# A second copy of V in DRAM with a pair's heads side by side, and gathers of random blocks from it

## Chip, cores and metric

One core of a Trainium2 chip runs the whole kernel. The metric is the device time of one execution in microseconds, taken as the median of several runs. Lower is better.

## The reference

Block-sparse attention (4 sequences, 8 heads, 768 positions, 64 features, blocks of 32) is followed by a mixture of 8 experts with one expert per token. Cut to what matters here:

```python
# q, k, v: (4, 8, 768, 64); sampled_blocks: (24, 3)
scores = scale * q @ k.T
mask = (|blk_i - blk_j| <= 1) | first or last block as query or key
for qb in range(24):
    for kb in sampled_blocks[qb]:
        mask[qb's 32 rows, kb's 32 columns] = True
attn = softmax(where(mask, scores, -1e9))
x = (attn @ v) as (3072, 512)
expert = argmax(normalized(x) @ normalized(expert_emb).T / tau)
out[t] = gate[t] * relu(x[t] @ w1[expert]) @ w2[expert]
```

Each block of 32 queries so reads its neighbours, the first and last block, and three random blocks of keys and values that are known only when the kernel runs.

## The kernel before, in words

The attention runs first, over chunks of 128 queries. Two sequences form a pair of sequences (`a` is 0 or 1), and the two chunks at the same place of such a pair form a pair of chunks: 12 of them (`NS`), which the text calls pair 0 to pair 11. A step of the loop in `attention_fast` (from line 1382) handles one chunk, so a pair takes two steps, and there are steps 0 to 24. In step `s` TensorE makes the scores of chunk `s` (L580 and L583 for the near keys, L605 for the random ones) and weighs the values of the chunk of the step before: `weigh_far` (L660 with the tile `vg`) for the random blocks, `weigh_near` (L660 with `st`) for the near ones. `normalize` then divides on VectorE and writes the tile `x` (L725), of which there are three buffers; `route` writes `x` to `x_dram` (L881) some steps later.

The values stand in SBUF in six tiles `vt[0]` to `vt[5]`, each of 128 partitions, and each partition holds one position: 2 sequences by 8 heads by 65 numbers, the 65th a one that makes the row sum. The tiles are loaded for `a` = 0 at the start and overwritten for `a` = 1 during the loop (`load_v`, `values_at`).

The random blocks of values come by DMA. `gather_v` (L484) yields, for each pair of chunks, 12 gathers (6 for the pairs 0 and 11, whose chunk holds only two blocks of this kind): for each of the three random slots `r` and each of the four query blocks `g`, 32 positions of both sequences and all heads go into 32 partitions of `vg`. The input has the heads far apart, so each gather is 512 pieces of 256 bytes. The start of the block is a register that SP reads (`shifts`). `lanes_of` picks the partitions: for `r` = 0 and 1 every second one from 32 to 95, for `r` = 2 32 neighbours. `vg` has two buffers, so the gathers of pair p are issued in the steps 2p-2 and 2p-1, the first of them behind `weigh_far` of step 2p-2, and their first reader is `weigh_far` of step 2p+1.

All these DMAs are issued by SP, in the order of the program: `fetch_all` (L493) puts one load (queries L497, keys L497, values L497) before every second gather (L499) and the loads that are left behind them (L501). The writes of `x` to `x_dram` follow at the end of a step. A wait at the head of this queue holds all that is behind it.

After the attention the expert tiles follow (L1218 and L1231), whose weights SP loads (L1171). The SBUF that they go to becomes free when the attention has ended.

Of the kernel before, what the change touches and what calls it, by code (L numbers as in the profile page):

```python
# [12 lines left out]
F32 = mybir.dt.float32  # L13
# [8 lines left out]
B, H, S, D = 4, 8, 768, 64  # L22
BLK = 32
NB = S // BLK
NRAND = 3
NC = S // P
# [24 lines left out]
VW = H * (D + 1)  # L51
NI = NB - 2
NCH = B * NC
DUO = 2
NS = NCH // DUO
TURNS = [0, 2, 1, 3, *range(4, NCH)]
DEN_LOW, DEN_HIGH = 0.1, 1e10
NEG = -1.0e9
LGAT = 80
# [260 lines left out]
def pieces(c, shifted=True):  # L320

    if not shifted:
        return [(slice(0, P), c * P)]
    if c:
        return [(slice(0, P), c * P - BLK)]
    return [(slice(0, BLK), S - BLK), (slice(BLK, P), 0)]
# [56 lines left out]
def lanes_of(slot, g):  # L383

    if slot < 2:
        return slice(BLK + slot, NRAND * BLK, 2)
    return slice(0, BLK) if (slot + g) % 2 == 0 else slice(NRAND * BLK, P)
# [16 lines left out]
def pair_chunk(s):  # L404

    a, at = divmod(s, NC)
    return a, at if a == 0 else (at + 1) % NC


def place(n):  # L410

    a, c = pair_chunk(n // DUO)
    return DUO * a + n % DUO, c, n % DUO


def of_seq(src, a, i=None):

    if i is None:
        return src[DUO * a:DUO * (a + 1)].rearrange("i h s d -> s (i h) d")
    return src[DUO * a + i].rearrange("h s d -> s h d")  # L420


def in_pair(t, i=None):

    return t.rearrange("p i h e -> p (i h) e") if i is None else t[:, i]
# [46 lines left out]
def blocks_of(c):  # L472

    return range(2 if c == 0 else 0, NG)
# [9 lines left out]
def gather_v(k, s, i=None):  # L484

    a, c = pair_chunk(s)
    t, src = k.vg_ring[s % 2], of_seq(k.v, a, i)
    for r in range(NRAND):
        for g, shift in zip(blocks_of(c), shifts(k, mybir.EngineType.SP, r, c)):
            yield in_pair(t[lanes_of(r, g), g], i)[:, :, 0:D], src[bass.ds(shift, BLK)]  # L490


def fetch_all(k, gathers, loads):  # L493

    for i, (to, src) in enumerate(gathers):
        if i % 2 == 0 and loads:
            k.nc.sync.dma_start(out=loads[0][0], in_=loads[0][1])  # L497
            loads = loads[1:]
        k.nc.sync.dma_start(out=to, in_=src)  # L499
    for to, src in loads:  # L500
        k.nc.sync.dma_start(out=to, in_=src)  # L501
# [785 lines left out]
def after_step(n, b):  # L1287

    s = TURNS.index(DUO * b + 1) + 2
    steps = route(n, b)  # L1290
# [18 lines left out]
def attention_fast(n, ctx):  # L1309
# [66 lines left out]

    turning = {0: (4, 5), 1: (6, 7), 10: (8, 9), 11: (10, 11, 12), 12: (13, 14, 15)}
    keys_at = {2: (8, 9), 3: (10,), 4: (11,), 5: (12,), 6: (13,), 10: (14, 15)}
    values_at = {7: (0,), 8: (1,), 9: (2,), 11: (3,), 13: (4,), 15: (5,)}
    routed = {TURNS.index(DUO * b + 1) + 2: b for b in range(NS - 1)}  # L1380
    plan = []
    for s in range(NCH + 1):
        now, after, last, past = (TURNS[i] if 0 <= i < NCH else None for i in (s, s + 1, s - 1, s - 2))
        if s in routed:
            plan = after_step(n, routed[s]) + [p for p in plan if p[0] >= s]

        def planned(half):
            for when, part, what in plan:
                if (when, part) == (s, half):
                    what()  # L1390

        def keys_gathered():
            if after is not None:
                gather_k(n, after)

        ends = last is not None and place(last)[1] == 0
        late_keys = s in turning and s > 0
        if now is not None:
            score_near(n, now)
            score_far(n, now)  # L1400
        if not late_keys:
            keys_gathered()
        summed, n.parted = n.parted, None
        if summed is not None:
            sum_logits(n, last)
        if past is not None and past >= 2 * DUO:
            turn_x(n, past)
        elif past is not None and past % DUO:
            turn_x(n, past - 1)
            turn_x(n, past)  # L1410
        if ends:
            score_ends(n, last, 0)
            score_ends(n, last, 2)
        elif after is not None:
            turn_q(n, after)
        for g in turning.get(s, ()):
            turn_k(n, g)
        if late_keys:
            keys_gathered()
        planned(0)  # L1420
        if s == 0:
            stack_ends(n, 1, (0, 1), 0)
            stack(n, 1, 0)
            near_v(n, 1, range(NG), 0)
        elif s == 2:
            stack_ends(n, 0, (1,), 1)
            stack(n, 0, 1)
            near_v(n, 0, range(NG), 1)
        elif s == 3:
            stack_ends(n, 1, (0, 1), 1)  # L1430
            stack(n, 1, 1)
            near_v(n, 1, range(NG), 1)
        elif s == 4:
            stack_ends(n, 0, (0,))
            stack(n, 2)
        elif s % 2 and 5 <= s < NCH:
            if s // DUO + 1 in (NC, NC + 1):
                stack_ends(n, s // DUO + 1, (0, 1))
            stack(n, s // DUO + 1)
        if last is not None:  # L1440
            for part in range(2):
                weigh_far(n, last, part)
        if past is not None and past % DUO:
            n.parted = past // DUO
            part_logits(n, n.parted)
        if ends:
            weigh_ends(n, last, (0, 2))
            score_ends(n, last, 1)
            score_ends(n, last, 3)
            if after is not None:  # L1450
                turn_q(n, after)
        ahead, odd = s // DUO + 1, s % DUO
        loads, gathers = [], ()
        if s in (2, 3):
            loads += load_q(n, s)
        elif s >= 4 and odd and ahead + 1 < NS:
            loads += load_q(n, ahead + 1)
        if s == 3:
            gathers = gather_v(n, ahead)
        elif s >= 4 and ahead < NS:  # L1460
            if not odd:
                coming = gather_v(n, ahead)
            gathers = coming if odd else islice(coming, 6)
        if s == 3:
            near_v(n, 2, (0, 1))
        elif s == 4:
            near_v(n, 2, (2, 3))
            near_v(n, 3, (0, 1))
        elif s > 4 and ahead < NS:
            near_v(n, ahead, (2, 3) if odd else (0, 1))  # L1470
        for g in keys_at.get(s, ()):
            loads += load_k(n, g)
        for m in values_at.get(s, ()):
            loads += load_v(n, 1, m)
        fetch_all(n, gathers, loads)
        if ends:
            weigh_ends(n, last, (1, 3))
        if last is not None:
            weigh_near(n, last, 0)
            weigh_near(n, last, 1)  # L1480
            normalize(n, last, summed)
        if s == 0:
            build_consts(n)
            next(experts)
        if s == 1:
            next(experts)
            setup.close()
            n.dp = pool("dp_e", 1)
        if s == NC * (B - 1):
            right.close()  # L1490
            n.wp = n.wp_ctx.enter_context(n.tc.tile_pool(name="wp", bufs=1, side="right", reuse_waits="tile"))
        planned(1)
# [159 lines left out]
@with_exitstack  # L1652
def kernel(
    ctx: ExitStack,
    tc: tile.TileContext,
    q: bass.AP,
    k: bass.AP,
    v: bass.AP,
    sampled_blocks: bass.AP,
    moe_expert_emb: bass.AP,  # L1660
    moe_tau: bass.AP,
    moe_w1: bass.AP,
    moe_w2: bass.AP,
    out: bass.AP,
):
    assert tuple(q.shape) == (B, H, S, D) and tuple(out.shape) == (N, DM)
    assert tuple(moe_w1.shape) == (E, DM, F) and tuple(sampled_blocks.shape) == (NB, NRAND)
    n = Net()
    n.tc, n.nc = tc, tc.nc
    n.q, n.k, n.v, n.blocks, n.out = q, k, v, sampled_blocks, out  # L1670
    n.emb, n.tau, n.w1, n.w2 = moe_expert_emb, moe_tau, moe_w1, moe_w2
    n.loaded, n.vs, n.es, n.ets, n.sums, n.x, n.rows, n.weights = {}, {}, {}, {}, {}, {}, {}, {}

    n.raw, n.nsq, n.lg, n.turned_rows, n.relu = {}, {}, {}, {}, None
    n.kt, n.qt, n.kg, n.pac, n.pd, n.pb, n.av, n.xt = ({} for _ in range(8))
    n.exact = n.attending = False
    n.const = ctx.enter_context(tc.tile_pool(name="const", bufs=1))
    n.x_dram = tc.dram_tile([N + 1, XW], F32, name="x_dram")
    n.dens = n.const.tile([P, NCH, H], F32, name="dens")

    fast(n)
    todo = n.nc.values_load(n.todo[0:1, 0:1], min_val=0, max_val=2)
    with tc.If(todo > 0):
        more(n)
# [32 lines left out]
```

## Time and profile before

| what | value |
|---|---|
| median of 3 runs | 625.15 us (624.96 to 627.76) |
| the profiled execution's own time | 619.32 us |
| its span, from the first to the last instruction | 617.6 us |
| TensorE busy | 583.4 us, 94% of the span |
| VectorE, ScalarE, GpSimd busy | 244.6, 146.4, 244.6 us |
| granted TensorE clock | 0.992 of full speed |
| DMA packets | 177073, of which 135432 under 512 bytes |
| HBM read, written | 156.65 MB, 12.90 MB |

The span divides into the attention (to about 250 us) and the experts. "Busy" counts the time in which an engine has an instruction under way, and TensorE's matmuls overlap, so its share says little on small stalls; the waits and the rows in order of time say more. The DMA share is the mean over 16 DMA engines of the time that their packets take, and can pass 1 where packets overlap.

### The profile page before, as it was taken

What the parts mean: (1) busy time and instruction counts of PE and PEld (TensorE: products, weight loads), DVE (VectorE), ACT (ScalarE), POOL (GpSimd) and SP (SyncE); (2) the same over time, 40 slices, a digit from 0 to 9 for tenths busy, and PEclk for the clock granted to TensorE, in tenths of its full rate; (3) what the DMA queues carried; (4) which work ended last, traced back from release to release, by engine and by line L of the source; (5) the groups of instructions that cost most, each with busy time, mean ns of one, the idle gap of its engine ahead of it and who ended that gap; (6) DMA issues with size and microseconds to landing.
All of it is one profiled execution on the core that took longest, in us unless ns stands there. A gap on an engine that the chain in (4) does not pass through costs nothing.

```text
span 617.6 us, 18763 instructions
## 1 busy us (share of the span) xinstructions
PE 583.4 (94%) x7732; PEld 451.8 (73%) x7732; DVE 244.6 (40%) x743; ACT 146.4 (24%) x287; POOL 244.6 (40%) x474
## 2 busy tenths in 40 slices
PE   7699999998989988999999999999999999999995
PEld 5588888887888977777766777755777636777772
DVE  4424667577879962457211121112122121121110
ACT  2346555565645544100000000000000000000000
POOL 2728347446766330320333334443333333334432
PEclk9799999999999999999999999999999999999999
DMA  9998798999999851899999999998999998999611
GB/s 201 235 171 192 150 169 179 187 198 210 199 196 203 180 193 39 266 402 393 406 400 392 408 396 324 340 327 307 404 408 390 398 381 309 395 400 408 226 36 35
DMA packets 177073, 170.60 MB, mean 276 GB/s; under 512 B 135432, under 2 KB 137608, under 8 KB 174162
## 3 DMA queue, kind: packets, MB, share of 16 engines
q1 hardware_dynamic: 170706, 155.61, 81.2%
q0 software_dynamic: 5216, 13.43, 6.0%
q8 instruction: 63, 1.03, 0.7%
q10 hardware_dynamic: 1056, 0.26, 0.2%
q14 instruction: 32, 0.26, 0.1%
HBM read 156.65 MB, written 12.90 MB: 275 GB/s over the span
## 4 chain that ended last, share of the span: by engine, by line
PE 75%; DVE 9%; DMA 5%; SPq 4%; ACT 2%; issue 2%; POOL 1%; POOLq 0%; DVEq 0%; ACTq 0%
PE hp L1218 26%; PE yp L1231 25%; PE av L660 7%; PE dps L605 4%; SPq L499 3%; PE hp L1263 2%; PE yp L1283 2%; DVE qt L549 2%; PE ac L580 2%; DMA vg<-in_v_dram 2%; DMA w<-in_moe_w_dram 2%; PE ac L583 2%; PE kps L526 1%; PE xg_ps L740 1%; DVE xt L743 1%
## 5 line engine op out<-in xcount | busy, mean ns | idle before, releaser
L1218 PEld LDWEIGHTS hp<-xgt,w 128*128 128x128 f32 x1472 | 167.8, 192 | 10.9 <-issue 10.2
L1218 PE MATMUL hp<-xgt,w 128*128 128x128 f32 x1472 | 169.2, 275 | 0.3 <-DMA w<-in_moe_w_dram 0.3
L1231 PE MATMUL yp<-w,h 128*128 128x512 f32 x368 | 162.0, 592 | 0.0
L1231 PEld LDWEIGHTS yp<-w,h 128*128 128x128 f32 x368 | 68.1, 190 | 76.6 <-issue 76.3
L1142 POOL DMA_INDIRECT xg<-x_dram,quarter x88 | 89.2, 1014 | 32.3 <-issue 27.4
L1244 POOL DMA_INDIRECT out_dram<-y,slot_l x20 | 20.5, 1023 | 156.0 <-DVE y L1243 156.0
L1221 ACT ACTIVATE h<-hp 128x512 f32<-128x512 f32 x23 | 13.7, 597 | 283.1 <-PE hp L1218 280.2
L1225 DVE TENSOR_SCALAR h<-hp 128x512 f32<-128x512 f32 x23 | 15.9, 691 | 126.8 <-PE hp L1218 126.8
L562 POOL COPY kg<-kt 128x128 f32 x176 | 43.8, 299 | 33.5 <-ACT kt L528 23.1
L1243 DVE TENSOR_SCALAR y<-yp,gate 128x512 f32<-128x512 f32 x20 | 15.0, 751 | 102.2 <-PE yp L1231 90.1
L511 POOL COPY vg<-vt 32x1040 f32<-32x1040 f32 (+1 forms) x45 | 43.1, 958 | 21.4 <-PE av L660 14.5
L605 PEld LDWEIGHTS dps<-qt,kg 128*64 128x64 f32 x1408 | 46.7, 138 | 0.0
L605 PE MATMUL dps<-qt,kg 128*64 128x64 f32 x1408 | 45.8, 222 | 0.0
L583 PE MATMUL ac<-qt,kt 128*64 128x256 f32 (+1 forms) x192 | 42.4, 364 | 1.2 <-ACT kt L536 1.2
L580 PE MATMUL ac<-qt,kt 128*64 128x128 f32 x352 | 42.8, 273 | 0.3 <-DVE qt L549 0.3
L580 PEld LDWEIGHTS ac<-qt,kt 128*64 128x64 f32 x352 | 37.9, 137 | 0.6 <-issue 0.5
L549 DVE COPY qt<-yp 64x512 f32<-64x512 f32 x48 | 32.8, 683 | 12.1 <-PE yp L544 11.7
L610 ACT ACTIVATE pd<-dps,bias 128x256 f32<-128x256 f32 x88 | 34.7, 476 | 8.5 <-PE dps L605 8.3
L660 PE MATMUL av<-vg,pd 128*32 128x65 f32 x1408 | 27.5, 221 | 4.1 <-DMA vg<-in_v_dram 2.0
L660 PEld LDWEIGHTS av<-vg,pd 128*32 128x32 f32 x1408 | 22.3, 109 | 8.8 <-issue 4.4
L660 PEld LDWEIGHTS av<-st,pac 128*64 128x64 f32 x704 | 22.8, 137 | 5.8 <-issue 4.8
L730 ACT ACTIVATE pac<-x 128x512 f32<-128x512 f32 x24 | 15.1, 631 | 49.5 <-DVE x L725 49.5
(244 smaller groups left out, 629.4 us busy)
## 6 DMA issues: line engine op xcount, KB each, us to landing
w<-in_moe_w_dram SPq DMA_DIRECT2D x52, 2048.0 KB, 15.2
vg<-in_v_dram SPq DMA_DIRECT2D x132, 128.0 KB, 4.4
kraw<-in_k_dram SPq DMA_DIRECT2D x32, 192.0 KB, 4.6
x_dram<-x SPq DMA_DIRECT2D x10, 516.0 KB, 5.2
qraw<-in_q_dram SPq DMA_DIRECT2D x9, 512.0 KB, 6.2
w<-in_moe_w_dram SPq DMA_DIRECT2D x8, 512.0 KB, 5.1
vt<-in_v_dram SPq DMA_DIRECT2D x10, 256.0 KB, 5.7
vt<-in_v_dram SPq DMA_DIRECT2D x5, 512.0 KB, 6.6
```

The source lines that it names most:

```text
L511: k.nc.gpsimd.tensor_copy(out=k.vg_ring[s % 2][lanes_of(NRAND, g), g, which(i)], in_=k.vt[m][rows, which(i)])
L549: k.nc.vector.tensor_copy(out=t[rows, :, h], in_=ps[rows])
L562: copy(out=t[:, :, g, lanes_of(s, g)], in_=kt[:, :, bass.ds(shift, BLK)])
L580: nc.tensor.matmul(out[0:D, j, half], lhsT=kt[:, j, at:at + D], rhs=qt[:, j, :, D * half:D * (half + 1)], start=True, stop=True)
L583: nc.tensor.matmul(out[D:P, j, half:2].rearrange("p f h t -> p h f t"), lhsT=kt[:, j, S:S + D], rhs=qt[:, j, :, D * half:P].rearrange("p h ...
L605: nc.tensor.matmul(out[D * r:D * (r + 1), NG * j + g], lhsT=kg[:, j, g, D * r:D * (r + 1)], rhs=qt[:, j, :, cols], start=True, stop=True)
L610: nc.scalar.activation(e[:, :, g].rearrange("p j h t -> p j (h t)"), out.rearrange("p (j g) h t -> p j g (h t)", g=NG)[:, :, g], ACT.Exp, ...
L660: k.nc.tensor.matmul(av[lanes, h // NPAIR, h % NPAIR * P:h % NPAIR * P + D + 1], lhsT=lhsT, rhs=rhs, start=first[0], stop=last, skip_group ...
L1142: k.nc.gpsimd.indirect_dma_start(out=x[:, g], out_offset=None, in_=quarters, in_offset=bass.IndirectOffsetOnAxis(ap=k.quarter[:, g, t:t + ...
L1218: nc.tensor.matmul(hp[:, f, :], lhsT=w1[:, d, (f0 + f) * P:(f0 + f + 1) * P], rhs=xt[:, d, :], start=(d == 0), stop=(d == ND - 1))
L1231: nc.tensor.matmul(yp, lhsT=h[:, f, :], rhs=w2[:, f, :], start=(f == 0), stop=(f == NF - 1))
L1244: k.scattered = nc.gpsimd.indirect_dma_start(out=k.out[:, :], out_offset=bass.IndirectOffsetOnAxis(ap=slot, axis=0), in_=y[:, :], in_offse ...
```

## The change

A DRAM tile `joined[a]` is added for each pair of sequences: 768 rows of 2 x 8 x 65 numbers, 4160 bytes each. `join_v` writes it from the six tiles `vt`, whole rows with the ones in them: for `a` = 0 at the end of step 3's DMAs, for `a` = 1 in step 12 (tiles 0 to 2) and step 13 (tiles 3 to 5). Tile 0 takes two DMAs, each other tile one. For the pairs 3, 4, 5, 8, 9, 10 and 11 the gathers read 32 whole rows of `joined` in place of 512 pieces of the input; 6 x 12 + 6 = 78 of the 132 gathers are of these pairs. The pairs 0, 1, 2, 6 and 7 gather as before. The values of `a` = 1 are loaded earlier, tile 2 in step 8 (was 9), tile 3 in 9 (was 11), tile 4 in 10 (was 13), tile 5 in 11 (was 15).

```diff
+JOINED = (3, 4, 5, 8, 9, 10, 11)
@@ def gather_v
-            yield in_pair(t[lanes_of(r, g), g], i)[:, :, 0:D], src[bass.ds(shift, BLK)]
+            if s in JOINED:
+                yield t[lanes_of(r, g), g].rearrange("p i h e -> p (i h e)"), k.joined[a][bass.ds(shift, BLK)]
+            else:
+                yield in_pair(t[lanes_of(r, g), g], i)[:, :, 0:D], src[bass.ds(shift, BLK)]
+
+def join_v(k, a, m):
+    rows_of = k.vt[m].rearrange("p i h e -> p (i h e)")
+    return [(k.joined[a][lo:lo + rows.stop - rows.start], rows_of[rows]) for rows, lo in pieces(m)]
@@ def attention_fast
-    values_at = {7: (0,), 8: (1,), 9: (2,), 11: (3,), 13: (4,), 15: (5,)}
+    values_at = {7: (0,), 8: (1, 2), 9: (3,), 10: (4,), 11: (5,)}
+    joined_at = {3: (0, range(NC)), 12: (1, range(3)), 13: (1, range(3, NC))}
...
         fetch_all(n, gathers, loads)
+        if s in joined_at:
+            a, some = joined_at[s]
+            fetch_all(n, (), [piece for m in some for piece in join_v(n, a, m)])
...
+    n.joined = [tc.dram_tile([S, DUO * VW], F32, name=f"joined{a}") for a in range(B // DUO)]
```

## Rows read from the trace of the kernel before

**Rows 1.** Windows: busy us (instructions) of PE, PEld, DVE, ACT, POOL; PEclk, DMA share, GB/s.

```profile
94.00:231.00 137.00, 124.95 (x3279) 113.38 (x3281) 107.34 (x350) 76.20 (x160) 76.79 (x208) 1.00 0.91 195
270.00:617.00 347.00, 340.35 (x1930) 235.94 (x1928) 78.05 (x190) 15.52 (x26) 114.02 (x114) 1.00 0.90 342
```

**Rows 2.** Waits from 50 to 231 us: waiter, releaser, us in total, times, longest.

```profile
PEld av L660 <- DMA vg<-in_v_dram: 3.0, 5, 1.3
DVE x L725 <- DMA x_dram<-x: 2.7, 1, 2.7
PE av L660 <- DMA vg<-in_v_dram: 2.0, 3, 1.1
```

**Rows 3.** Timeline of PE: weigh_far of steps 7, 9, 13, 15 and 19 (start, us, ...).

```profile
94.40 1.11 PE L660 MATMUL av<-vg,pd 128*32 128x65 f32 x64
...
110.69 0.31 PE L660 MATMUL av<-vg,pd 128*32 128x65 f32 x4
112.11 1.21 PE L660 MATMUL av<-vg,pd 128*32 128x65 f32 x59 [1.10 <-DMA vg<-in_v_dram]
...
150.38 0.73 PE L660 MATMUL av<-vg,pd 128*32 128x65 f32 x4 [0.29 <-DMA vg<-in_v_dram]
...
167.29 1.20 PE L660 MATMUL av<-vg,pd 128*32 128x65 f32 x59 [0.57 <-DMA vg<-in_v_dram]
...
200.29 1.01 PE L660 MATMUL av<-vg,pd 128*32 128x65 f32 x57 [0.58 <-issue]
```

**Rows 4.** The page's DMA issues: KB of one, median us from issue to landing.

```profile
vg<-in_v_dram SPq DMA_DIRECT2D x132, 128.0 KB, 4.4
...
vt<-in_v_dram SPq DMA_DIRECT2D x5, 512.0 KB, 6.6
```

**Rows 5.** Timeline of SP's queue: six gathers of slots 0 and 1, three of slot 2.

```profile
149.19 4.74 SPq L499 DMA_DIRECT2D vg<-in_v_dram  x6
...
126.43 1.43 SPq L499 DMA_DIRECT2D vg<-in_v_dram  x3
```

**Rows 6.** Window of 1 us while SP issues only gathers (columns as Rows 1).

```profile
211.00:212.00 1.00, 1.00 (x17) 1.00 (x15) 0.93 (x4) 0.00 (x0) 0.00 (x0) 1.00 0.61 140
```

**Rows 7.** Timeline of SP's queue: the gather behind a load of queries, then of values.

```profile
155.25 1.48 SPq L499 DMA_DIRECT2D vg<-in_v_dram  x1
...
158.59 3.23 SPq L499 DMA_DIRECT2D vg<-in_v_dram  x1
```

**Rows 8.** Timeline of SP's queue from step 3's last gathers to step 6's end.

```profile
62.04 6.49 SPq L499 DMA_DIRECT2D vg<-in_v_dram  x8
68.92 0.40 SPq L497 DMA_DIRECT2D kraw<-in_k_dram  x1
72.00 1.46 SPq L499 DMA_DIRECT2D vg<-in_v_dram  x2
...
85.22 1.92 SPq L499 DMA_DIRECT2D vg<-in_v_dram  x2
...
95.72 2.03 SPq L881 DMA_DIRECT2D x_dram<-x  x2
```

**Rows 9.** DMA from 239 to 246 us, forty slices: one write to DRAM alone.

```profile
GB/s 0 0 0 0 0 0 0 0 0 0 12 389 366 366 377 389 377 366 319 47 24 24 12 94 0 0 0 0 0 0 0 0 0 0 0 0 0 0 0 0
...
x_dram<-x SPq DMA_DIRECT2D x1, 516.0 KB, 3.4
```

**Rows 10.** Timeline of DVE and SP: normalize in steps 7 and 15, a write.

```profile
101.30 0.69 DVE L725 TENSOR_TENSOR x<-av,inv 128x512 f32<-128x512 f32 x1 [2.73 <-DMA x_dram<-x]
...
163.71 1.56 SPq L881 DMA_DIRECT2D x_dram<-x  x1
...
170.55 0.69 DVE L725 TENSOR_TENSOR x<-av,inv 128x512 f32<-128x512 f32 x1
```

**Rows 11.** Waits of SP's queue over the whole span.

```profile
SPq L1171 <- PE av L660: 8.6, 1, 8.6
```

**Rows 12.** The page's line of DMA packets.

```profile
DMA packets 177073, 170.60 MB, mean 276 GB/s; under 512 B 135432, under 2 KB 137608, under 8 KB 174162
```

## The prediction, made before the changed kernel was built or run

> **What bounds the kernel now.** I read the windows by stage first. From 270 us on TensorE is busy for 340 of 347 us, at full granted clock, and the change touches nothing there. From 94 to 231 us it is busy for 125 of 137 us while the DMA engines are at 0.91 [rows 1], so the attention has two bounds that lie close together. Which one ends last is seen in the waits: in the attention TensorE waits on gathers of values for 3.0 us at the weight load and 2.0 us at the matmul (the same stalls, seen twice), and VectorE once for 2.7 us on a write of `x` [rows 2]. In order of time, `weigh_far` takes 1.11 us where nothing is late (step 7). In step 9 it begins at 110.69 us, stands still after four matmuls and ends 1.21 us after 112.11: 2.63 us, 1.5 too long. The steps 13, 15 and 19 show the same, with 1.4, 1.4 and 0.8 us lost from first matmul to last; one row of each stands there [rows 3]. These 5.1 us, and 0.8 us of TensorE in step 8 behind VectorE's wait, are all that a faster way to fetch V can give back. What is late there is not one transfer, since a gather lands 4.4 us after its issue [rows 4], but SP's queue: the gathers of pair 6, for step 13, go out until 147 us and are read from about 150 us on.
>
> **What a gather costs that queue.** Six gathers of slots 0 and 1, back to back, take 4.74 us, 0.79 each; three of slot 2, whose lanes are neighbours, 1.43 us, 0.54 each with the gap behind them [rows 5]. Both kinds move 512 pieces. So twelve that wait for nothing hold SP for 8 x 0.79 + 4 x 0.54 = 8.5 us. While SP does only this, the DMA engines are at 0.61 [rows 6]: there the issue sets the pace and not the bytes. Behind a load of queries the next gather holds SP for 1.48 us, behind one of values for 3.23 us [rows 7], for there the engines are full.
>
> **What a joined gather saves.** 32 rows instead of 512 pieces. Its lanes are those of before. Lower bound for its issue: 0.54 us, the price with neighbouring lanes; upper bound: 0.79, if every second lane is what costs. Eight a pair save 0 to 2.0 us; I take 1, between them. Further, the transfers of these gathers no longer stand in the engines ahead of the loads. A gather takes the engines about 0.61 x 0.79, 0.5 us; joined, 133 KB at the 400 GB/s or so of the largest slices of a write [rows 9] take 0.33 us. The wait behind a load of values should fall from 3.23 to about 2.1 us (two gathers stand between it and the queries), that of the write of `x` from 1.56 us [rows 10] to 0.5, that behind the queries by 0.3. Together S = 1 + 1.1 + 1.1 + 0.3 = 3.5 us of SP's time for each joined pair, with bounds of 1.4 (the last two alone) and 6 (an issue of 0.54, and no wait behind the values). A load that is not joined stays as it was, and the loads are the larger part of the packets.
>
> The Trainium skill (DMA: Bandwidth & Descriptors, section Specifications) gives 512 bytes as the least size for full rate. By it the gathers would be bound by their 256-byte pieces; the engines at 0.61 in [rows 6] speak against that for this queue, and what would follow from it is the first rival.
>
> **What the writes cost, and what stands behind them.** One write of 516 KB with nothing beside it moves at about 375 GB/s and lands 3.4 us after its issue, so 2.0 us are not bytes [rows 9]. The tile `joined[0]` is 768 x 4160 bytes = 3.19 MB: 8.5 us at that rate. Step 3's last gather leaves SP at 68.5 us [rows 8]. The seven writes follow, and the first joined gather, in step 4, reads what they write, so SP has to wait until they have landed: 68.5 + 2.0 + 8.5 + about 1 for what is still in the engines = 80 us, where before the first gather went at 72.0 us [rows 8]. Only one load of keys goes ahead of it. Everything else on SP, the gathers of the pairs 3 and 4, the queries, the keys, and the first two writes of `x`, stands behind this wait. So +8.0 us in the queue. For `joined[1]` it is 1.6 MB in each of the steps 12 and 13, 4.3 us each, and in step 14 a wait of some 6 us again, where by then no reader is near.
>
> **Moved loads.** Tiles 4 and 5 now come ahead of the last gathers of pair 6, before only behind them. At about 3.0 us each (3.23 less the next gather's own share, plus its own issue) that is +6.0 us for pair 6, and -3.0 us again by pair 7, from which tile 4 is gone. Tiles 2 and 3 change steps but not sides. The writes of `x` in steps 7, 9, 11 and 13 are moved by whatever stands ahead of them. The DMAs go by SP alone; TensorE, VectorE, ScalarE and GpSimd get no instruction more or less.
>
> **The sum, at each place where TensorE meets the queue.** How late SP is, against before:
> - Step 7: pair 3 has +8.0 - 3.5 = +4.5 us on its last gather. Before it was issued until 87.1 us [rows 8] and read at 94.40 [rows 3], so it lands near 95.5 us: +1 us.
> - Step 8: the write of `x` from step 6 has +8.0 - 1.5 x 3.5 = +2.8 us. VectorE already waited for it in step 7 until 101.30 us [rows 10], and TensorE was 0.8 us late behind that, so all of it is felt: +2.8 us, with the +1 inside it.
> - Step 9: pair 4 is +1 in the queue and TensorE +2.8, so the stall of 1.5 us is gone.
> - Step 13: +8.0 - 3 x 3.5 + 6.0 = +3.5 us; TensorE, now about 1.5 late by itself, waits to +3.5.
> - Step 15: +3.5 - 3.0 + 4.3 (tiles 0 to 2, which now stand ahead of pair 7's second half) = +4.8 us. The write of `x` behind it also has tiles 3 to 5 ahead of it; it had about 1.7 us to spare (issued from 163.71 us, needed at 170.55 [rows 10]), so some +5.
> - After that five pairs of joined gathers, without loads of values, leave SP time in hand: the stall of 0.8 us in step 19 goes.
>
> +5 - 0.8 = about +4 us at the end of the attention. The weights of the first experts wait for TensorE's last `weigh` there [rows 11], so the experts move by the same amount. In bounds: with S = 6 step 13 is at 8 - 18 + 6 = -4 and no step is late any more; with S = 1.4 step 15 is at 8 - 4.2 + 6 - 3 + 4.3 = +11.
>
> The profiled execution took 619.32 us (617.6 us of span and 1.7 around it): 623 us by this sum. The median of the runs is 625.15 us, 5.8 above it, and I move that by the same 4 us: 629 us.
>
> **Rivals.**
> 1. *Faster.* The queue is set by the 512 pieces after all, S is 5.5 or more, and the eight microseconds of step 3 are worked off before step 7. Then all stalls named above go: -5.1 - 0.8, about -6 and some of it given back, 620 us. It decides from S = 5.1, where 15.3 - 3S (step 15) turns negative. For it: the gathers behind values are held for 3.23 us, and after the change 39,936 of the 135,432 small packets [rows 12] are gone. Against it: [rows 5] and [rows 6], where the pace is the same with the engines 0.39 idle. This is also the time that the rule of the Trainium skill cited above would give, and the section Rules for kernel authors of the same page has a sentence for coalescing many small transfers.
> 2. *No change.* The wait for the writes and the moved loads cost what the gathers save, S between 4 and 5.1: 622 to 627 us. For it: SP was idle for 2.7 us ahead of 72.0 us anyhow [rows 8], and TensorE's lag hides what SP loses.
> 3. *Much slower.* The writes run at half of the rate of a single write, since keys and queries share the engines with them: +8.5 us at step 8 and +4 at step 15, of which most is felt, about +12, 637 us. For it: values landed after 6.6 us in the crowded queue [rows 4] against 3.4 for a larger write alone [rows 9].
> 4. *The change does not do what it says*: the rows of 4160 bytes are cut into pieces. Then the packet count would not fall by 36,000; the time would be that of rival 3. Little speaks for it.
>
> **Chances.** The forecast 0.42, rival 1 0.25, rival 2 0.20, rivals 3 and 4 0.13. A difference of under 0.5%, 3.1 us, is about what cannot be told from none in a measurement of this kernel. Part of the forecast's own range (626 to 634 us) lies within it, so: faster 0.25, same 0.27, slower 0.48. The range over the cases goes from 618 (all stalls gone, and a little more) to 638 us.
>
> **What would show it.** SP's queue should have no gather from about 72 to 80 us, and again some 6 us ahead of step 14's; if it has them at 72 us, the +8 is wrong. Joined gathers of slots 0 and 1 should follow each other at 0.55 to 0.8 us; at 0.54 and with the gather behind values under 1.5 us, S is near 6 and rival 1 wins. TensorE's waits on `vg` should move from step 9 to the steps 7 or 8, 13 and 15, and VectorE's on the write of `x` grow past 2.7 us. The packets under 512 bytes should be 95,496. The expert stage should keep its length; if it changes, I have missed something.

## The result, and the profile after

The changed kernel takes 632.12 us, median of 7 runs (630.33 to 635.83), against 625.15 us for the kernel before beside it (7 runs, 623.24 to 627.76). The ratio is 1.0138 with a 95% interval of 1.0109 to 1.0166, so about 8.6 us of 625 (6.8 to 10.4): slower, and about twice the 4 us that were forecast. The two medians alone lie 7.0 us apart, at the low end of that.

The two traces lie further apart than the medians. The profiled execution after took 635.5 us, at the slow end of its seven, and the one before 619.32, at the fast end. So 16 us lie between the traces, and a difference read from them is large by up to a factor of two, in its late part above all. 1.4 us are lost before step 4, where nothing of the change has run yet: `weigh_far` of step 4 begins at 72.31 us, before at 70.87. The granted clock of the first 60 us is 0.91, before 0.94. These rows of after and of before are windows (columns as in [rows 1]).

```profile
0.00:60.00 60.00, 47.52 (x978) 41.10 (x980) 25.52 (x94) 25.14 (x46) 28.45 (x99) 0.91 0.96 200
```

```profile
0.00:60.00 60.00, 50.14 (x1007) 43.28 (x1008) 25.52 (x94) 25.50 (x46) 30.15 (x100) 0.94 0.97 200
```

I take 1.4 us off the lateness of every later step, and call what is left "net". It compares with a kernel before that starts as late; SP itself is only 0.1 us late at the end of step 3 (68.65 us below, 68.53 before).

The change does what it says. The page of after (compare [rows 4, 12]) has 78 gathers of 130 KB and, of the writes, ten of a whole tile, and the small packets fell to 95,720; 95,496 were forecast.

```profile
DMA packets 141393, 177.15 MB, mean 280 GB/s; under 512 B 95720, under 2 KB 97896, under 8 KB 138482
...
vg<-joined SPq DMA_DIRECT2D x78, 130.0 KB
...
joined<-vt SPq DMA_DIRECT2D x10, 520.0 KB
```

SP's queue in order of time (compare [rows 8]; start, us held, what was issued). It is held by the seven writes for 7.3 us, issues one load of keys, and then stands until the first joined gather at 81.34 us, where before it went on at 72.00.

```profile
68.65 7.33 SPq L511 DMA_DIRECT2D joined<-vt  x7
76.79 0.40 SPq L507 DMA_DIRECT2D kraw<-in_k_dram  x1
81.34 1.19 SPq L509 DMA_DIRECT2D vg<-joined  x2
...
93.63 1.09 SPq L509 DMA_DIRECT2D vg<-joined  x2
...
101.17 1.01 SPq L891 DMA_DIRECT2D x_dram<-x  x2
...
160.77 3.29 SPq L511 DMA_DIRECT2D joined<-vt  x4
...
173.60 1.93 SPq L511 DMA_DIRECT2D joined<-vt  x3
175.64 1.13 SPq L891 DMA_DIRECT2D x_dram<-x  x1
180.53 1.83 SPq L509 DMA_DIRECT2D vg<-joined  x2
```

Who waits (60 to 250 us; us in total, times, longest; compare [rows 2]): TensorE for gathers, 6.2 us at the matmul where it was 2.0; VectorE for the write of `x`; and, new, SP for the landing of the copy.

```profile
PE av L670 <- DMA vg<-in_v_dram: 5.1, 7, 1.8
PE av L670 <- DMA vg<-joined: 1.1, 1, 1.1
...
PEld av L670 <- DMA vg<-joined: 1.9, 4, 1.2
...
DVE x L735 <- DMA x_dram<-x: 4.4, 2, 3.6
...
SPq L509 <- DMA joined<-vt: 7.2, 3, 3.5
```

In order of time, `weigh_far` of the steps 7, 13 and 15 (first and last rows of each; compare [rows 3]). Step 7 was on time before and now lasts from 96.45 to 100.45 us. Step 15 begins at 174.60 us and ends at 178.38, 7.2 and 8.4 us net later than before.

```profile
96.45 0.69 PE L670 MATMUL av<-vg,pd 128*32 128x65 f32 x4 [0.53 <-issue]
98.21 2.13 PE L670 MATMUL av<-vg,pd 128*32 128x65 f32 x59 [1.07 <-DMA vg<-joined]
...
156.37 0.69 PE L670 MATMUL av<-vg,pd 128*32 128x65 f32 x4 [1.55 <-DMA vg<-in_v_dram]
...
157.98 1.01 PE L670 MATMUL av<-vg,pd 128*32 128x65 f32 x57 [0.26 <-DMA vg<-in_v_dram]
...
174.60 0.27 PE L670 MATMUL av<-vg,pd 128*32 128x65 f32 x2 [1.83 <-DMA vg<-in_v_dram]
...
176.52 1.75 PE L670 MATMUL av<-vg,pd 128*32 128x65 f32 x57 [0.27 <-DMA vg<-in_v_dram]
```

The last row holds something that the forecast has no term for: 57 matmuls take 1.75 us where 57 take 1.01 in step 13. The windows of 5 us show why: in the third column from the end the granted clock is below 1 here. In four of the windows with a lower clock it comes behind a window in which TensorE was idle for 1.5 to 2 us; behind the one from 155 us, with 2.1 us idle, it does not.

```profile
95.00:100.00 5.00, 3.28 (x70) 2.64 (x73) 4.42 (x14) 3.61 (x7) 2.67 (x11) 0.81 0.95 219
100.00:105.00 5.00, 5.00 (x111) 4.19 (x102) 0.37 (x2) 0.37 (x1) 4.63 (x13) 0.85 0.71 177
...
155.00:160.00 5.00, 2.90 (x92) 2.06 (x94) 2.10 (x7) 2.87 (x6) 2.29 (x8) 1.00 0.86 225
160.00:165.00 5.00, 5.00 (x116) 4.93 (x113) 3.75 (x12) 2.53 (x6) 4.88 (x10) 1.00 0.89 237
...
170.00:175.00 5.00, 3.04 (x67) 2.59 (x63) 4.19 (x16) 4.23 (x8) 0.97 (x5) 1.00 0.74 154
175.00:180.00 5.00, 4.03 (x86) 2.98 (x88) 0.17 (x1) 0.82 (x2) 4.29 (x11) 0.66 1.06 379
...
235.00:240.00 5.00, 5.00 (x140) 4.79 (x140) 1.59 (x7) 0.18 (x2) 0.00 (x0) 0.70 0.45 178
...
255.00:260.00 5.00, 5.00 (x176) 4.64 (x172) 0.55 (x2) 1.62 (x2) 0.00 (x0) 0.66 0.13 48
```

In the trace of before no window of 5 us from 85 to 290 us has a clock below 1.00; it is the only one of the traces here without such a window. The last `weigh_far` begins at 256.66 us, before at 242.74: 12.5 us net. The experts add 1.3 us, one window of theirs being at 0.74.

### The profile page after: what moved, and what is told of

The parts are those of the page before. It is cut to its first block, busy times and chain, and to the rows that moved or that the text cites. A ratio compares the mean times of both kernels' runs of the same rounds, so it can differ in the third digit from the quotient of the medians.

```text
span 633.7 us, 18780 instructions
## 1 busy us (share of the span) xinstructions
PE 590.7 (93%) x7732; PEld 457.6 (72%) x7732; DVE 240.8 (38%) x743; ACT 146.0 (23%) x287; POOL 244.5 (39%) x474
## 2 busy tenths in 40 slices
DMA packets 141393, 177.15 MB, mean 280 GB/s; under 512 B 95720, under 2 KB 97896, under 8 KB 138482
## 4 chain that ended last, share of the span: by engine, by line
PE 77%; SPq 7%; DVE 4%; DMA 4%; issue 3%; ACT 2%; POOL 1%; another core or an unknown queue 1%; POOLq 0%; DVEq 0%; ACTq 0%
PE hp L1228 25%; PE yp L1241 24%; PE av L670 8%; SPq L509 5%; PE dps L615 4%; PE hp L1273 2%; PE yp L1293 2%; PE ac L590 2%; PE ac L593 2%; PE xg_ps L750 1%; DMA w<-in_moe_w_dram 1%; PE bps L646 1%; PE kps L536 1%; DVE qt L559 1%; ACT pb L648 1%
## 5 line engine op out<-in xcount | busy, mean ns | idle before, releaser
L1228 PEld LDWEIGHTS hp<-xgt,w 128*128 128x128 f32 x1472 | 169.4, 193 | 11.4 <-issue 10.2
L670 PE MATMUL av<-vg,pd 128*32 128x65 f32 x1408 | 31.2, 235 | 8.1 <-DMA vg<-in_v_dram 5.1
L559 DVE COPY qt<-yp 64x512 f32<-64x512 f32 x48 | 32.8, 684 | 11.8 <-PE yp L554 11.4
L620 ACT ACTIVATE pd<-dps,bias 128x256 f32<-128x256 f32 x88 | 34.6, 476 | 9.0 <-PE dps L615 9.0
L670 PEld LDWEIGHTS av<-vg,pd 128*32 128x32 f32 x1408 | 25.3, 118 | 13.5 <-issue 8.5
L670 PE MATMUL av<-st,pac 128*64 128x65 f32 x704 | 27.5, 230 | 0.8 <-issue 0.7
```

The lines of the kernel that those rows point to most:

```text
L559: k.nc.vector.tensor_copy(out=t[rows, :, h], in_=ps[rows])
L620: nc.scalar.activation(e[:, :, g].rearrange("p j h t -> p j (h t)"), out.rearrange("p (j g) h t -> p j g (h t)", g=NG)[:, :, g], ACT.Exp, ...
L670: k.nc.tensor.matmul(av[lanes, h // NPAIR, h % NPAIR * P:h % NPAIR * P + D + 1], lhsT=lhsT, rhs=rhs, start=first[0], stop=last, skip_group ...
L1228: nc.tensor.matmul(hp[:, f, :], lhsT=w1[:, d, (f0 + f) * P:(f0 + f + 1) * P], rhs=xt[:, d, :], start=(d == 0), stop=(d == ND - 1))
```

## Experiments

Each ran beside the kernel before; lateness in us is the ratio's excess times the median of before on that chip. The plain difference of the medians departs from it by up to 1.8 us. I began with a theory Q: SP's queue is a sum, TensorE waits for the queue's order, and the forecast missed only sizes in it. Its rivals are named in each expectation.

### The moved loads alone (e1_moved)

```diff
-    values_at = {7: (0,), 8: (1,), 9: (2,), 11: (3,), 13: (4,), 15: (5,)}
+    values_at = {7: (0,), 8: (1, 2), 9: (3,), 10: (4,), 11: (5,)}
```

> The kernel before with one part of the change alone: the values of a = 1 are loaded at the earlier steps; no writes to joined, no joined gathers. Theory Q (SP's queue in order: a load of 2048 pieces holds it for some 3 us, so tile 2 now stands ahead of pair 5's last gathers and the tiles 4 and 5 ahead of pair 6's): slower than before by 4 to 5 us, about 0.7%, with TensorE waiting on vg some 2 us in step 11 and until 4 us later than before in step 13. Rival B (what costs is the 6.4 MB that the writes put on the DMA engines): no byte more, so within 1 us of before.

Measured: 627.01 us against 623.10, ratio 1.0058 (1.0025 to 1.0091), 3.6 us slower. As Q has it. Step 9 lasts 2.81 us, much as before (2.68), but the steps 11 and 13 last 2.37 and 3.46 (before 1.11 and 2.58): there is a load more ahead of pair 5 too, which the forecast denied.

### The writes and the moved loads, no reader (e2_writes)

```diff
-JOINED = (3, 4, 5, 8, 9, 10, 11)
+JOINED = ()
```

> The changed kernel with JOINED empty: the writes to joined and the moved loads stand, all gathers read the input as before, so nobody waits for the writes. Theory Q: the writes hold SP for about 7 us in step 3 and 3 us each in the steps 12 and 13 by their issue alone, and the 1.5 to 2.5 us a pair that joined gathers gave are gone: 10 to 14 us slower than before, more than the changed kernel's 8.6. Rival W (the wait for the landing of the writes is what costs, 9 us at step 4): without it the time falls to that of the moved loads alone, 4 to 5 us over before.

Measured: 635.07 us, ratio 1.0197 (1.0163 to 1.0232), 12.3 us slower. As Q has it. So all that the 78 joined gathers give, with the waits that they bring, is 12.3 less 8.6, some 4 us, with about 2 us of uncertainty on either number.

### No one waits for the copy (e3_no_wait)

```diff
-JOINED = (3, 4, 5, 8, 9, 10, 11)
+JOINED = (4, 5, 9, 10, 11)
```

> The changed kernel with JOINED = (4, 5, 9, 10, 11): the pairs 3 and 8, whose gathers come right behind the writes, read the input, so SP has two steps for other work before it needs the written rows and the wait for their landing should be gone. Theory Q: the 4.2 and 3.8 us in which SP stood still go, and the 1.7 us that pair 3 saved go with them: 4 to 6 us over before instead of 8.6. Rival B (bytes on the engines): as the changed kernel, 8 to 9 us over before.

Measured: 631.93 us, ratio 1.0165 (1.0104 to 1.0225), 10.3 us slower. Q falls here. SP no longer waits for the landing and issues pair 3's first gather at 77.30 us in place of 81.34, but the first writes of `x` come at 100.20, only 1 us earlier than in the changed kernel, of which 0.7 is an earlier start (the seven writes at 67.91 against 68.65). Its SP queue:

```profile
67.91 7.25 SPq L511 DMA_DIRECT2D joined<-vt  x7
75.95 1.11 SPq L507 DMA_DIRECT2D kraw<-in_k_dram  x1
77.30 1.83 SPq L509 DMA_DIRECT2D vg<-in_v_dram  x2
...
100.20 1.00 SPq L891 DMA_DIRECT2D x_dram<-x  x2
```

The wait that the forecast priced at 8 us is not where the time goes: without it the queue is late anyway. Two things changed at once here, since the pairs 3 and 8 lost their savings with their wait, and 10.3 us (6.5 to 14.0) cannot be told from 8.6; the writes without any reader, further down, are the cleaner test.

### The first half alone (e4_first)

```diff
-JOINED = (3, 4, 5, 8, 9, 10, 11)
+JOINED = (3, 4, 5)
-    values_at = {7: (0,), 8: (1, 2), 9: (3,), 10: (4,), 11: (5,)}
-    joined_at = {3: (0, range(NC)), 12: (1, range(3)), 13: (1, range(3, NC))}
+    values_at = {7: (0,), 8: (1,), 9: (2,), 11: (3,), 13: (4,), 15: (5,)}
+    joined_at = {3: (0, range(NC))}
```

> Only the first half of the change: joined for a = 0, its writes in step 3, the pairs 3, 4 and 5 gathered from it; the loads of a = 1 where they were before, nothing joined for a = 1. Theory Q: TensorE is 3 to 4 us late at step 8 (SP waits until about 81 us and the first writes of x come behind that), but the pairs 5 to 7 are no later than before, so the stalls of the steps 9, 13 and 15 are covered by it: 1 to 3 us over before. Rival B: about half of the 8.6 us, 4 us, as half of the bytes are written.

Measured: 628.82 us, ratio 1.0083 (1.0046 to 1.0119), 5.2 us slower, more than either had it. The stalls of the steps 9 to 19 shrink (13 and 15 last 1.11 us each, before 2.58 and 2.53), as three joined pairs should make them, and yet the loss of the steps 7 and 8 is not won back.

### The second half alone (e5_second)

```diff
-JOINED = (3, 4, 5, 8, 9, 10, 11)
+JOINED = (8, 9, 10, 11)
-    joined_at = {3: (0, range(NC)), 12: (1, range(3)), 13: (1, range(3, NC))}
+    joined_at = {12: (1, range(3)), 13: (1, range(3, NC))}
```

> The moved loads and the second half of the change: joined for a = 1 alone, written in the steps 12 and 13, the pairs 8 to 11 gathered from it; pairs 3 to 5 read the input and nothing is written in step 3. Theory Q, mended by the first runs (what counts is how late SP is at the places where TensorE needs it; the writes hold SP by their bytes whether or not anyone waits for them): the moved loads alone gave 3.9 us; the writes of tiles 0 to 2 put pair 7 about 4 us later, those of 3 to 5 the write of x behind it, so TensorE is 3 to 5 us later in step 15 than with the moved loads alone: 6 to 9 us over before, granted clock about 0.981. Rival A (the parts add up: 8.6 for all, less 5.2 for the first half, less 3.9 for the moved loads): the second half costs nothing, 3 to 4.5 us over before.

Measured: 631.08 us against 623.92, ratio 1.0100 (1.0052 to 1.0148), 6.2 us slower. The halves give 5.2 + 6.2 = 11.4 us, the whole 8.6. That a step that is late already hides what comes late with it would explain the rest, but each of these numbers is uncertain by 2 to 3 us, so whether the halves add up is not shown.

### The copy written from another queue (e6_act_queue, e7_act_45)

Both issue the writes from ScalarE's queue; the second joins only the pairs 4 and 5, with the loads of before.

```diff
-            fetch_all(n, (), [piece for m in some for piece in join_v(n, a, m)])
+            for piece in [piece for m in some for piece in join_v(n, a, m)]:
+                nc.scalar.dma_start(out=piece[0], in_=piece[1])
```

> The changed kernel with the writes to joined issued from ScalarE's queue instead of SP's; everything else as changed, so the joined gathers of the pairs 3 and 8 still wait until the rows have landed. Theory Q (hold): SP is free of the 7 us of issue in step 3 but waits for the landing at step 4 as before, to about 80 us; in the steps 12 and 13 it is free and pair 7 and the writes of x come 3 to 5 us earlier than in the changed kernel: 4 to 7 us over before. Rival B (bytes): the engines carry the same 6.4 MB at the same places, 8 to 9 us over before.

Measured: 634.86 us, ratio 1.0173 (1.0124 to 1.0223), 10.8 us slower (7.7 to 13.9), no better than the change. The first writes of `x` go out at 102.29 us.

```profile
102.29 1.00 SPq L891 DMA_DIRECT2D x_dram<-x  x2
```

> First half without hold and without wait: joined for a = 0 is written from ScalarE's queue in step 3, only the pairs 4 and 5 are gathered from it, two steps later, and the loads of a = 1 stand where they were before. SP neither issues the writes nor waits for them; the engines still carry the 3.2 MB. Theory Q: the two pairs' savings (1.5 to 2.5 us each) come without their price, SP is earlier by 2 to 4 us in the steps 9 to 13, and the time is 0 to 4 us under before. Rival B (bytes): the 8.5 us of the write stand in the engines ahead of pair 3 and of the first writes of x, TensorE is 3 us or more late in step 8, and the time is 2 to 4 us over before.

Measured: 629.77 us, ratio 1.0090 (1.0059 to 1.0121), 5.6 us slower. The same as the first half from SP (5.2). But neither kernel frees SP. ScalarE issues the copy from 63.00 us on, ahead of step 3's gathers, and SP stands 8.6 us between a load of keys and its next gather, at 69.11 us. That gather reads the input, and yet it waits for the copy (SP's waits, 60 to 250 us, of the second kernel; 12.4 in the first):

```profile
SPq L509 <- DMA joined<-vt: 8.9, 2, 8.4
```

The cause lies in how these kernels count their DMAs. In the traces, in the semaphore numbers of the issuing instructions, the DMAs of SP and ScalarE tell their landing on the same eight semaphores (counters that an engine can wait for), and each is issued only when the last one on its semaphore has landed. The gather at 69.11 us takes the semaphore of the third write of the copy, which ScalarE issued at 63.87 us and which landed at 68.98. From SP alone the eight go round in order, and in the kernel before SP waits for no DMA between 60 and 250 us. So the theory's condition, an SP that neither issues nor waits, did not hold, and these two runs do not decide between Q and B.

### Another load from another queue (e9_q_act)

The kernel before, with the loads of queries from step 5 on issued by ScalarE.

```diff
-            loads += load_q(n, ahead + 1)
+            queries = load_q(n, ahead + 1)
+        for to, src in queries:
+            nc.scalar.dma_start(out=to, in_=src)
```

> The kernel before, nothing of the change; the loads of queries from step 5 on are issued from ScalarE's queue instead of SP's. If the place where the time is lost is SP's queue in order, so that a load of 2048 pieces holds the gathers behind it, SP gains 1.5 to 2.5 us per pair, TensorE's stalls of the steps 9, 13, 15 and 19 shrink, and the kernel is 2 to 6 us faster than before, with a higher granted clock (0.990). If the engines are the bound, the bytes are the same and the time stays within 1.5 us.

Measured: 632.15 us against 623.92, ratio 1.0103 (1.0052 to 1.0154), 6.4 us slower; neither had that. The chain of waits of that stretch (start, us, what) shows the queries' transfer and the write of `x` that comes in behind it; VectorE waits 8.5 us for that write, before 2.7.

```profile
96.69 6.56 DMA qraw<-in_q_dram
103.25 0.02 issue
103.27 3.50 DMA x_dram<-x
```

SP's waits (60 to 250 us) show that this is again the shared semaphore: SP holds back gathers and the write of `x`, which need nothing from the queries, until queries of ScalarE's queue have landed, nine times and for 34.6 us in all.

```profile
SPq L499 <- DMA qraw<-in_q_dram: 24.9, 7, 7.1
...
SPq L501 <- DMA qraw<-in_q_dram: 5.7, 1, 5.7
...
SPq L881 <- DMA qraw<-in_q_dram: 4.0, 1, 4.0
```

So a second queue didn't open a free path in these kernels, and the three runs don't tell what one would give whose DMAs SP need not wait for. The Trainium skill (DMA: Bandwidth & Descriptors, section "Issuing engines are not separate DMA queues") says that DMAs of all engines run on the same 16 DMA engines and interleave, and that issuing from several only saves issue time. No run here isolates that.

### The gathers without their price (e10_gain, e12_no_write)

Both read fixed rows of one tile that one DMA writes; the first has the loads of before, the second the moved loads of the change.

```diff
-                yield t[lanes_of(r, g), g].rearrange("p i h e -> p (i h e)"), k.joined[a][bass.ds(shift, BLK)]
+                yield t[lanes_of(r, g), g].rearrange("p i h e -> p (i h e)"), k.joined[0][g * BLK:(g + 1) * BLK]
-    joined_at = {3: (0, range(NC)), 12: (1, range(3)), 13: (1, range(3, NC))}
+    joined_at = {3: (0, (1,))}
```

> The joined gathers without their price: the loads are those of the kernel before, one DMA of one tile (128 rows, 0.53 MB) stands where seven stood, and the gathers of the pairs 3, 4, 5, 8, 9, 10 and 11 read 32 fixed rows of that tile. It leaves out the copying of V and the addresses of the blocks, so other numbers are weighed and other experts picked; the attention's steps are what to compare. Theory Q (a joined gather frees SP's queue by some 2.5 us a pair, as the gaps between the last gathers of each pair in the changed kernel say, and the queue's order is what TensorE waits for): the stalls of the steps 9, 13, 15 and 19 go, last weigh_far 4 to 6 us earlier than before, 4 to 6 us faster. Theory E (the other loads keep the engines as busy, so that the gathers' gain is not felt): within 1.5 us of before, the stalls of the steps 13 and 15 still over 2 us long from first to last matmul.

Measured: the whole took 657.87 us, but with other experts picked, so only the attention speaks. No DMA wait of TensorE over 0.2 us is left between 60 and 250 us, and the `weigh_far` of the steps 9, 13 and 15 take 1.11 us each; that of step 13:

```profile
148.14 1.11 PE L670 MATMUL av<-vg,pd 128*32 128x65 f32 x64
```

Step 16 begins at 174.53 us, before at 177.00; with 0.85 us of late start (step 4) taken off, 3.3 us earlier. But the last `weigh_far` begins at 243.07 us, before at 242.74, 0.5 us earlier net. The stalls went as Q says, the 4 to 6 us did not come. Part of the reason is in SP's waits (60 to 250 us), of before and then of this kernel: SP, served sooner, waits for TensorE to free `vg`, and a lead can't be stored past its two buffers.

```profile
SPq L499 <- PE av L660: 3.7, 6, 1.2
```

```profile
SPq L509 <- PE av L670: 17.1, 9, 4.4
...
SPq L509 <- PE dps L615: 4.3, 1, 4.3
```

The clock takes its part. The window from 175 to 180 us is at 0.66 behind a wait of 1.8 us for VectorE; before had the same wait (1.7 us) and kept 1.00. From step 16 to step 17 it takes 8.4 us, before 6.8. At step 20 the lead is 2.7 us again, and the last 2.1 us go behind it: the windows from 220 to 230 us are at 0.85 and 0.81, and from step 22 to step 23 it takes 7.8 us, before 6.6.

```profile
175.00:180.00 5.00, 5.00 (x108) 4.91 (x98) 2.19 (x10) 0.90 (x3) 3.82 (x10) 0.66 0.62 158
```

> The kernel of e10_gain with the moved loads of the change (tile 2 in step 8, 3 in 9, 4 in 10, 5 in 11): everything but the writes. It leaves out the copying of V and the addresses of the blocks, as there. Theory Q (all parts are sums in one queue): the gain of 4 to 6 us less some of the 3.9 us that the moved loads cost by themselves, so 0 to 4 us faster than before, and the change's loss is all due to the writes. Theory E (the loads set the pace whatever the gathers do): 3 to 4 us slower than before, as with the moved loads alone.

Measured: 657.93 us, again with other experts. Step 13 has a stall (2.88 us from first to last), all other steps to 21 take 1.11 to 1.12, and the last `weigh_far` begins at 244.45 us: 0.4 us later than before, net of 1.3. So with joined gathers the moved loads cost 1 us or less, not the 3.6 that they cost alone; the rest of what the changed kernel loses, some 12 us in its trace, comes with the writes. Q's range for the sum, 0 to 4 us faster, is missed by 0.4 us, in one trace.

### The writes alone, in a row and one by one (e11_write1, e13_spread)

The kernel before with the copy for `a` = 0 and no reader: seven writes in step 3, or one tile a step.

```diff
-JOINED = (3, 4, 5, 8, 9, 10, 11)
+JOINED = ()
-    joined_at = {3: (0, range(NC)), 12: (1, range(3)), 13: (1, range(3, NC))}
+    joined_at = {3: (0, range(NC))}
```

> The kernel before with the seven writes of joined[0] at the end of step 3 and no reader, loads as before. Theory Q (the writes cost what they hold SP, 7.3 us less the 2.7 us that SP was idle there): 4 to 7 us slower than before, stalls in the steps 7 and 8, as much as the kernel that also joins the pairs 3, 4 and 5 or more. Theory W (in that kernel the loss of 5.2 us came from SP's wait for the landing of the writes): 0 to 2 us slower.

Measured: 627.05 us against 621.93, ratio 1.0080 (1.0052 to 1.0109), 5.0 us slower, W falls. That is what the first half costs with its three joined pairs (5.2 us): as far as these two numbers tell, their gathers pay for the wait that they bring, and for nothing else. VectorE waits 6.1 us for the write of `x` at the end of step 7, TensorE begins step 8 behind it, and the clock falls:

```profile
DVE x L735 <- DMA x_dram<-x: 6.1, 1, 6.1
```

```profile
105.00:115.00 10.00, 6.36 (x116) 5.89 (x118) 3.95 (x14) 3.38 (x8) 3.00 (x9) 0.66 1.08 196
```

In the other kernel the writes stand one tile a step:

```diff
-    joined_at = {3: (0, range(NC))}
+    joined_at = {3: (0, (0,)), 4: (0, (1,)), 5: (0, (2,)), 6: (0, (3,)), 7: (0, (4,)), 8: (0, (5,))}
```

> The same 3.2 MB as in the kernel with the seven writes of joined[0] in a row and no reader (5.1 us slower than before), but one tile a step at the end of the steps 3 to 8; loads as before. Theory B (the bytes cost what they take the DMA engines, 8.5 us at the rate of a single write, wherever they stand, since the engines are at 0.91): 4 to 7 us slower than before again. Theory L (what hurts is the row of seven at one place, 7.3 us of SP ahead of pair 3's gathers; single writes of about 1 us go into the gaps of 2.7 us and more in which SP waits for vg to come free): 0 to 2 us slower.

Measured: 628.73 us against 623.09, ratio 1.0111 (1.0060 to 1.0161), 6.9 us slower: B holds, L falls. Each write now holds SP for 0.4 to 0.6 us only and pair 3's first gather goes out on time (73.05 us, 1.1 of them late start). But the gathers behind the writes are held longer: the write of `x` goes out at 100.49 us, 3.7 late net, and VectorE waits even longer (6.69 us) for it. The rows are SP's queue, then VectorE.

```profile
79.18 0.61 SPq L511 DMA_DIRECT2D joined<-vt  x1
91.28 0.36 SPq L511 DMA_DIRECT2D joined<-vt  x1
99.78 0.61 SPq L511 DMA_DIRECT2D joined<-vt  x1
100.49 1.31 SPq L891 DMA_DIRECT2D x_dram<-x  x2
```

```profile
107.03 0.69 DVE L735 TENSOR_TENSOR x<-av,inv 128x512 f32<-128x512 f32 x1 [6.69 <-DMA x_dram<-x]
```

So the 3.2 MB of the first copy cost 5 to 7 us in each of four forms: in a row with readers that wait (e4, 5.2) or with none (e11, 5.0), one tile a step (e13, 6.9), and from ScalarE's queue (e7, 5.6). What is common to them is that the transfers stand ahead of others, and that SP issues the first write of `x` late, by 3.7 to 7.1 us net. Whether they cost by the queue that they hold or by the engines that they fill is not separated, since no run left SP on time. That they fill the DMA engines is not shown: the mean DMA share from 60 to 110 us is 0.82 with the spread writes and 0.86 before. A kernel with a fourth buffer of `x`, which would take its write off VectorE's path, was not run either, so how much of the cost goes by that write stays open.

## Why the prediction was right in its direction and wrong in its size

Two terms of the sum failed. S, the saving of a joined pair, was entered three times at 3.5 us, 10.5 in all, and gave 7.5 behind the copy. And the end of the attention behind step 15 was entered at -0.8 us and lost 4.1 in the trace. The clock had no term at all; by correlation some 2 us of the medians go with it. That the direction came out is in part luck: the 8 us were booked to a wait, and the writes cost 5 us without it.

- *The wait for the copy: right in size, wrong as the cause.* The first joined gather was forecast for 80 us and went at 81.34; that is +7.9 us net where +8.0 were entered. But the kernel without that wait is no faster (e3), and the writes without a reader cost 5.0 us (e11): there pair 3's first gather goes at 76.93 us, 4.3 late net, and the write of `x` at 102.11, 5.8 late net, with nobody waiting for the copy.
- *Step 8: the right path, too low.* +2.8 us were forecast by way of the write of `x`, VectorE and TensorE. The write went out 4.0 us late net (101.17 against 95.72), VectorE waited 3.61 us for it and TensorE began step 8 3.8 us late net. One trace doesn't fix this: e4 has the same instructions up to there and begins step 8 at 111.38 us, 6.5 late net.
- *S, the term that was mis-sized first.* I took 3.5 us for each joined pair and added it up three times. Pair 3's twelve gathers, with the loads between them, take 15.1 us before (72.00 to 87.14, [rows 8]) and 11.8 in e10 (72.96 to 84.79), so S is 3.3 where no copy is written: the estimate was good. Behind the copy they take 13.4 (81.34 to 94.72), S = 1.7; by the lateness of their last gathers the pairs 4 and 5 give 3.7 and 2.1, the latter with 3.0 us allowed for the load that now stands ahead of pair 5. That is 7.5 us where 10.5 were forecast. The 3.0 us missing are the whole difference at pair 6: its last gather is 6.4 us late net, forecast 3.5. The issue of a joined gather (0.47 us and a gap of 0.2) lay within the stated bounds.
- *"Tiles 2 and 3 change steps but not sides": wrong.* With tile 2 in step 8 and tile 3 in step 9, one load more stands ahead of pair 5 (e1: step 11 lasts 2.37 us, before 1.11). It doesn't change the sum at pair 6, where two loads more were counted.
- *Steps 13 and 15: too low.* +3.5 and +4.8 were forecast; they end 5.2 and 8.4 us late net. SP's wait ahead of step 14's gathers, forecast at some 6 us, is the gap of 3.8 us ahead of 180.53 us.
- *After step 15: the missing term.* I expected 0.8 us back. Between step 15 and the end of the attention another 4.1 us were lost. The windows at 175, 235 and 255 us are at 0.66, 0.70 and 0.66 of the clock: at most 5 x (0.34 + 0.30 + 0.34) = 4.9 us, so the clock can account for all of the 4.1; that it does is not shown. The stall of step 19 did go, as forecast (1.11 us).
- *The same term in the medians.* The seven runs after have a mean clock of 0.980; four sets of the kernel before have 0.985 to 0.987. Within the sets of seven runs and more, one of the kernel before apart (2.9 to 3.9 in the others), a run is some 3.5 us longer for each 0.01 less of clock. So about 2 of the 8.6 us go with the clock. That is a correlation; that the stalls lower the clock is the likely reading, and no run shows it apart. With the 3.0 us of S, 4 + 3 + 2 = 9 comes near the 8.6 measured.
- *The expert stage* keeps its length but for the 1.3 us named above. The rivals: the faster case (620 us) would have needed the stalls to be worth 6 us; with the gathers nearly for free they are worth 3.3 at step 16 and 0.5 at the end of the attention (e10). The 512 pieces were not the bound. The much slower one priced the writes at half rate, 8.5 us more; the first joined gather, which waits for them, came 1.3 us behind the forecast that had them at full rate.

In short: the writes of the first half alone cost 5 to 7 us, with or without a reader that waits; what the gathers give is eaten by the wait, by two buffers and by the clock. Even with the gathers nearly for free the attention ends only 0.5 us earlier, in one trace each. The trace of before lies 5.8 us under its kernel's median and that of e10 1.9 us, so some 4 us more are possible; even that would not repay a copy whose first half alone costs 5.

## What to carry to other kernels

Price a transfer that is added to a crowded stage by its bytes ahead of whatever is waited for next, not by the wait that it creates: taking that wait away or spreading the writes gained nothing here. Before a transfer is moved to another queue, see in the waits whether the first queue still waits for its landing; here it did, for up to 8.5 us at a time, and nothing was gained. A saving for each step may be summed only as far as the buffers let the queue run ahead; past that it turns into waits of the queue (3.7 to 17.1 us here). And where TensorE gets stalls of some microseconds, count what the granted clock may take behind them as a term of its own.

## What the runs showed of the hardware

- *The clock.* Behind some stalls the granted clock fell: 0.66 from 175 to 180 us after TensorE had been idle for 2 of the 5 us before, with matmuls at 1.75 us for 57 in place of 1.01, which is the lower of the two levels (1.2 GHz against 2.4) for most of the window. Not each stall does it: from 155 to 160 us TensorE was busy for only 2.9 us, and the window behind it is at 1.00. The Trainium skill (TensorE: Matmul & The Clock Gate, section "HAM oscillation — how this bites in real kernels") tells of waits for DMA that lower the clock; these traces agree in that the fall at 175 us comes behind waits for gathers, and show it in a kernel that keeps TensorE busy for 93% of the span.
- *Issue on SP.* A gather of 32 rows of 4160 bytes holds SP for 0.47 us into every second partition and 0.32 into neighbours; one of 512 pieces for 0.60 and 0.35. Fewer pieces saved 0.13 and 0.03 us of issue, neighbouring partitions 0.25 (512 pieces) and 0.15 (32 rows). In e10, whose gathers read fixed rows, the 32 rows take 0.54 and 0.42.
- *A second queue.* Three kernels that moved transfers to ScalarE's queue (e6, e7, e9) were 5.6 to 10.8 us slower than the kernel before; in e9 nothing else was changed. In all three SP waited for landings of ScalarE's DMAs that its own work did not need (8.4 us at a time in e7, 34.6 us in all in e9), so they tell of semaphores that two queues share and not of what a second queue can carry.
